# Gate/up units taken two by two in a one-core transformer block

## The chip, the cores and the metric

The kernel runs on one core of one Trainium2 chip. The metric is the device time of one execution in microseconds. Engines are called PE (TensorE; PEld is its weight load), DVE (VectorE), ACT (ScalarE), POOL (GpSimd) and SP (the engine whose queue issues the DMAs).

## The reference

One block with modulated layer norms: linear attention, then a gated feed-forward. The change lies in the feed-forward's gate and up projections. S = 2048 tokens, D = 1024, F = 3584; all inputs are bfloat16.

```python
phi = lambda t: jnp.where(t > 0, t + 1, jnp.exp(t)) + 1e-06
# linear attention A: 32 heads, num / den of phi(q), phi(k), v, then @ wo
mod = (_silu(c) @ w_mod).reshape(c.shape[0], 6, 1, -1)
sa, ca, ga, sb, cb, gb = ...
h = _layernorm(x) * (1 + ca) + sa
x = x + ga * A(h, A_wqkv, A_wo)
h = _layernorm(x) * (1 + cb) + sb
x = x + gb * (gelu(h @ w_gate) * (h @ w_up) @ w_down)
```

## The kernel before

After attention come output chunks (`wo_chunk`, 128 rows each) and then the gate/up stage, 28 units. Unit u works on half p = u // 14 of the tokens (1024 of them) and on 256 of the 3584 columns of `w_gate` and of `w_up`. Each unit is a 2 x 2 block product with seven products instead of eight (the Strassen-Winograd scheme): products 1 and 2 take the blocks as they are, in bfloat16; products 3 to 7 take sums of blocks, held in float32r. Every product is made twice, for t = 0 (gate) and t = 1 (up), with 4 matmuls of 128x128 by 512 columns each (`prod`, L1458). So a unit has 16 bfloat16 and 40 float32r matmuls, in the order 1, 2, 6, 5, 7, 3, 4.

The names and lines that matter:

- The sums of token blocks (`SS`, `s_sum`, L1413) are made once per half. The sums of weight blocks (`TP[0]` to `TP[4]`, `t_sum`) are made in each unit: numbers 0, 1, 2, 4 on DVE (L1433), number 3 is a copy on ACT (`brcp`, L1423). Sum 0 belongs to product 5, 1 to 6, 2 to 7, 3 to 3, 4 to 4; each has one buffer, so a sum for the next unit waits for the product that reads the old one. Units 1 to 27: sums 2 and 4 of the unit itself are queued behind its first product, sums 0, 1 and 3 of the next unit behind products 5, 7 and 3.
- PSUM has eight banks; a unit uses four pairs of them (t = 0 and 1): `BA` for products 1 and 2, `BB`, `BE`, `BC`. Product 1 is copied from `BA` to `BB` by ACT (`pcp`, L1463), and product 2 then adds onto `BA`. Product 6 adds onto `BB`, and `ucp` (ACT, L1473) copies that to `BC`. Product 5 goes to `BE`, from there to SBUF (`escp`, ACT, L1466), and `pinc` (DVE, L1476) adds it to `BC`. Product 7 adds onto `BB`, and `padd` (DVE, L1469) sums `BB` and the copy into `BE`. Products 3 and 4 add onto `BC` and `BB`. All four pairs then hold gate (t = 0) and up (t = 1) of one output block.
- `gelu` (ACT, L1481) takes the gate bank into one of two buffers `ge`; `y_out` (DVE, L1488) multiplies it with the up bank into `ys`. The last `y_out` of a unit is held back until the next unit's first product has been issued. `y_store` (SP, L1494) writes `ys` out.
- `wt_dma(u + 2)` loads the next but one unit's weights into one of two buffers, gate and up 512 KB each (SP, L1371). Before, it is queued behind product 2, and waits for the sums that read the old weights.
- Work for other stages is hooked into the units. `ACTS` holds, for units 2 to 11, two groups of ACT steps: squares with a running sum (`ln2_stats`, L674), followed on POOL by `ve`, `rs` and `nm` (L676, L677, L679), normalizations (`ln2_rows`, L660, which need `rs` and `nm`, and a DMA transpose after them), modulations (`act_mod`, L753) and copies. `DVES` holds POOL means, DVE sums (`s_sum`) for the second half of the tokens, and from unit 15 on the weight sums `d_t` (L1621) of the down projection. `DMAS` holds loads and stores. Before, the DMAs, the `DVES` step and the first ACT group stand behind a unit's product 2, the second ACT group behind product 5.
- Units 0 and 27 have orders of their own; unit 27 carries the first steps of the down projection (`d_t`, `d_s`, `d_first`).

Each engine's queue is in program order; what waits for what is worked out from the bytes and banks that the steps touch. A planner (`Sched.reorder`) rearranges DVE, ACT and POOL alone, and only in the stretch from output chunk 3 to the end of unit 1.

Of the kernel before, what the change touches and what calls it, by code (L numbers as in the profile page):

```python
# [7 lines left out]
ACTF = mybir.ActivationFunctionType  # L8
ALU = mybir.AluOpType

P = 128
# [12 lines left out]
NFP = NFC // 2  # L24
# [10 lines left out]
OFF_YT = OFF_HT + NSG * 8192  # L35
# [295 lines left out]
def bass_adaLN_cond__linear_attn_block__geglu_ffn__prompt_kernel(  # L331
# [18 lines left out]
    with ExitStack() as es:  # L350
# [6 lines left out]
        def at(name, shape, dty, off):  # L357
            return nc.alloc_sbuf_tensor_at(name, shape, dty, offset=ABASE + off, align_bytes=4)
# [28 lines left out]
        YS = [at(f"ys{i}", [P, CPG, 2, 2 * P], bf16, OFF_YS[i]) for i in range(3)]  # L387
        YA = [at(f"ya{r}", [P, NDJ, 2 * P], bf16, o_) for r, o_ in enumerate(OFF_YA)]
        DE = at("de", [P, 512], f32, OFF_DE)
        PK = [at(f"pk{i}", [P, D], bf16, OFF_PK[i]) for i in range(NCH)]  # L390
        MB = [at(f"mb{i}", [P, D], bf16, OFF_MB[i]) for i in range(NG)]
        MTB = [at(f"mtb{i}", [P, NDC, P], bf16, OFF_MTB[i]) for i in range(2)]
# [141 lines left out]
        def r_2k(off, name):  # L534
            return [(off, off + 2048, name)]
# [16 lines left out]
        sch = Sched()  # L552
# [815 lines left out]
        def wt_dma(u):  # L1368
            i, f0 = u % 2, u % NFP * 256
            for t, v_ in enumerate((wg_v, wu_v)):  # L1370
                sch.dma(Q, lambda e, t=t, v_=v_: e.dma_start(WT[i][:, t, :, :], v_[:, :, f0:f0 + 256]), wr=r_wt(i, t, t + 1), note=f"wt{t} u{u}")  # L1371

        def wo_chunk(c_, b0):
            wo_mm(c_, b0, list(range(NG)))
# [58 lines left out]
            sch.op(V, lambda e: e.tensor_tensor(TP[k][:], in0, in1 if k in (0, 2) else in1[:], ALU.subtract), rd=r0 + r1, wr=r_tp(k),  # L1433
                   deps=[x1_ops[7]] if u == 0 and k == 0 else [], note=f"tsum{k} u{u}")

        BA, BE, BB, BC = 0, 2, 4, 6
        gi = [0]

        def prod(u, t, k):
            p = PS_[0] = u // NFP  # L1440
            if k in (1, 2):
                r = k - 1
                lhs = lambda dc: (WT[u % 2][:, t, r * ND2 + dc, 0:P], r_wt(u % 2, t, t + 1, r * ND2 + dc, r * ND2 + dc + 1))
                rhs = lambda dc: (H2[p][0][:, r * ND2 + dc, :], r_h2(0, r * ND2 + dc, r * ND2 + dc + 1))
            else:
                ti = {5: 0, 6: 1, 7: 2, 3: 3, 4: 4}[k]
                lhs = lambda dc: (TP[ti][:, t, dc, :], r_tp(ti, t, t + 1))
                if k == 4:
                    rhs = lambda dc: (A22R[p][:, dc, :], r_ar(dc, dc + 1))
                else:  # L1450
                    si = {5: 0, 6: 1, 7: 2, 3: 3}[k]
                    rhs = lambda dc: (SS[p][si][:, dc, :], r_ss(si, dc, dc + 1))
            b = {1: BA, 2: BA, 5: BE, 6: BB, 7: BB, 4: BB, 3: BC}[k] + t
            fresh = k in (1, 5)
            o = None
            for dc in range(ND2):
                (l_, rl), (r_, rr) = lhs(dc), rhs(dc)
                o = sch.op(T, lambda e, l_=l_, r_=r_, dc=dc: e.matmul(PS(b), l_, r_, start=fresh and dc == 0, stop=dc == ND2 - 1, skip_group_check=True),  # L1458
                           rd=rl + rr, pwr=(pr(b) if dc == 0 else ()), note=f"ffn u{u} P{k} {t} dc{dc}", overwrite_ok=True)
            pset_writer(b, o)  # L1460

        def pcp(t):
            sch.op(A, lambda e: e.activation(PS(BB + t), PS(BA + t), ACTF.Copy), prd=pr(BA + t), pwr=pr(BB + t), note="pcp")  # L1463

        def escp(t):
            sch.op(A, lambda e: e.activation(ES[t][:, :], PS(BE + t), ACTF.Copy), prd=pr(BE + t), wr=r_2k(OFF_ES[t], f"es{t}"), note="escp")  # L1466

        def padd(t, dst):
            sch.op(V, lambda e: e.tensor_tensor(PS(dst + t), PS(BB + t), ES[t][:, :], ALU.add), prd=pr(BB + t), rd=r_2k(OFF_ES[t], f"es{t}"),  # L1469
                   pwr=pr(dst + t), note="padd")  # L1470

        def ucp(t):
            sch.op(A, lambda e: e.activation(PS(BC + t), PS(BB + t), ACTF.Copy), prd=pr(BB + t), pwr=pr(BC + t), note="ucp")  # L1473

        def pinc(t):
            sch.op(V, lambda e: e.tensor_tensor(PS(BC + t), PS(BC + t), ES[t][:, :], ALU.add), prd=pr(BC + t), rd=r_2k(OFF_ES[t], f"es{t}"),  # L1476
                   pwr=pr(BC + t), note="padd")

        def gelu(b):
            i = gi[0] % 2  # L1480
            sch.op(A, lambda e: e.activation(GE[i][:, :], PS(b), ACTF.Gelu_apprx_tanh), prd=pr(b), wr=r_2k(OFF_GE[i], f"ge{i}"), note="gelu")  # L1481
            gi[0] += 1
# [14 lines left out]

        held = [None]

        def unit(u, order=(1, 2, 6, 5, 7, 3, 4)):  # L1500
            more = u + 1 < 2 * NFP
            for k in order:
                if isinstance(k, tuple):
                    wo_chunk(*k)
                    continue
                if callable(k):
                    k()
                    continue
                late = u == 0 and k == 2
                gb_, gk, yt, yh = (None, 1, 0, 0) if late else {2: (BA, 0, 0, 0), 7: (BE, 1, 1, 1), 3: (BC, 0, 1, 0), 4: (BB, 0, 0, 1)}.get(k, (None, 1, 0, 0))  # L1510
                for t in range(2):
                    prod(u, t, k)
                    if k == 1:
                        if held[0]:
                            held[0]()
                            held[0] = None
                        pcp(t)
                    elif k == 5:
                        escp(t)
                        if u:  # L1520
                            pinc(t)
                    elif k == 6:
                        if u:
                            ucp(t)
                        else:
                            padd(t, BC)
                    elif k == 7:
                        padd(t, BE)
                    if gb_ is not None and t == gk:
                        gelu(gb_)  # L1530
                        ig = (gi[0] - 1) % 2
                if k == 2 and u + 2 < 2 * NFP:
                    wt_dma(u + 2)
                if k == 4:
                    def last(ig=ig):
                        y_out(ig, BB, u, 0, 1)
                        y_store(u)
                    held[0] = last
                elif gb_ is not None:
                    y_out(ig, gb_, u, yt, yh)  # L1540
                if k == 1:
                    if u == 0:
                        ar_copy(0)
                    else:
                        if u == 1:
                            t_sum(u, 1)
                        t_sum(u, 2)
                        t_sum(u, 4)
                if more:
                    if k == (3 if u == 0 else 5):  # L1550
                        t_sum(u + 1, 0)
                    if k == 7 and u:
                        t_sum(u + 1, 1)
                    if k == 3:
                        t_sum(u + 1, 3)
# [242 lines left out]
        def lat(*f):  # L1798
            return lambda: [g() for g in f]
# [34 lines left out]
        for u in range(2 * NFP):  # L1834
            if u == 0:
                unit(u, ORD0)
            elif u == 2 * NFP - 1:
                unit(u, (1, lambda: (d_t(0, 3), d_s(0, 0, (0,)), d_s(0, 1, (0,))), 2, lambda: (wd_dma(4), wd_dma(5)), 6, 5, 7,
                         lambda: (d_t(1, 3), d_s(0, 0, (1,)), d_s(0, 1, (1,))), 3, lambda: (wd_dma(6), x_in(0, 0, 1, 2, 3)), d_first, lambda: (d_t(2, 3), d_t(3, 3)), 4))
# [3 lines left out]
            if u == 1:  # L1843
                mark.append(sch.n)
        held[0]()
        held[0] = None
        def hook0(k):
# [137 lines left out]
```

## Time and profile before

| what | value |
|---|---|
| median of 3 runs | 782.76 us (782.47 to 783.43) |
| span of the profiled execution | 780.9 us |
| PE busy / DVE busy / ACT busy | 770.2 / 645.9 / 374.6 us |
| granted PE clock | full in every slice |
| gate/up matmuls (L1458), share of the chain that ended last | 45% |
| one steady unit | 12.56 us, in it DVE 10.80 to 11.93, ACT 6.73 busy |

The span runs from the first to the last instruction of one execution; the profile page gives no other time of that execution, and the median of the runs stands 1.9 us above its span. A busy time is the union of an engine's instructions; matmuls overlap, so their spacing from start to start, and not their duration, tells what PE can do.

### The profile page before, as it was taken

How to read it: one execution, taken by the hardware profiler on the slowest of the kernel's cores; microseconds unless marked ns; L12 is line 12 of the kernel's file. 1: busy time of each engine (PE TensorE's matmuls, PEld its weight loads, DVE VectorE, ACT ScalarE, POOL GpSimd, SP SyncE). 2: the span in 40 equal slices, each digit the busy share in tenths (PEclk: the TensorE clock that was granted, in tenths of full speed). 3: DMA queues.
4: the chain of work that ended last, by engine and by line, in shares of the span. 5: the costliest groups of instructions: out<-in, count | busy, mean ns of one | idle time of the engine just before them, and what ended most of it. 6: DMA issues, size and time to landing. Idle time of an engine off the chain costs nothing.

```text
span 780.9 us, 10753 instructions
## 1 busy us (share of the span) xinstructions
PE 770.2 (99%) x3825; PEld 496.2 (64%) x3883; DVE 645.9 (83%) x964; ACT 374.6 (48%) x629; POOL 47.5 (6%) x126
## 2 busy tenths in 40 slices
PE   8999999999999999999999999999999999999998
PEld 4444445666445667667676767667676576677766
DVE  6699988897899878787989888888989888676767
ACT  2497743242466487878755555555555211111111
POOL 2031300000321011100000000000000000000000
PEclk9999999999999999999999999999999999999999
DMA  9879749939999358867353865535356334443331
GB/s 284 256 167 252 158 91 215 255 80 196 203 287 231 82 138 212 230 175 215 99 145 108 250 211 172 148 96 161 97 147 221 111 127 139 144 141 114 126 125 60
DMA packets 196940, 130.22 MB, mean 167 GB/s; under 512 B 69516, under 2 KB 182420, under 8 KB 195864
## 3 DMA queue, kind: packets, MB, share of 16 engines
q1 hardware_dynamic: 196872, 129.55, 62.4%
q8 instruction: 30, 0.49, 0.3%
q14 instruction: 22, 0.18, 0.1%
q10 hardware_dynamic: 16, 0.00, 0.0%
HBM read 92.55 MB, written 23.35 MB: 148 GB/s over the span
## 4 chain that ended last, share of the span: by engine, by line
PE 95%; SPq 2%; DMA 1%; DVE 1%; issue 1%; ACT 0%; DVEq 0%; ACTq 0%
PE ps_all L1458 45%; PE ps_all L1672 21%; PE ps_all L895 7%; PE ps_all L934 7%; PE ps_all L1283 7%; PE ps_all L880 5%; PE ps_all L1593 1%; SPq L598 1%; DMA wmq<-in_w_mod_dram 1%; SPq L603 1%; DMA h1T<-xh 0%; PE ps_all L913 0%; PE ps_all L1201 0%; PE ps_all L1240 0%; DVE h1T L724 0%
## 5 line engine op out<-in xcount | busy, mean ns | idle before, releaser
L1458 PE MATMUL ps_all<-ss,tp 128*128 128x512 f32 x896 | 214.3, 396 | 0.0
L1458 PEld LDWEIGHTS ps_all<-ss,tp 128*128 128x128 f32 x896 | 168.3, 188 | 37.8 <-DVE ss L1413 0.2
L1672 PE MATMUL ps_all<-dt,sb 128*128 128x512 f32 x424 | 102.5, 398 | 0.0
L1481 ACT ACTIVATE ge<-ps_all 128x512 f32<-128x512 f32 x112 | 64.1, 597 | 73.8 <-DVE ps_all L1469 62.1
L1458 PE MATMUL ps_all<-h2a,wt 128*128 128x512 bf16 x421 | 95.7, 379 | 1.8
L1672 PEld LDWEIGHTS ps_all<-dt,sb 128*128 128x128 f32 x424 | 79.6, 188 | 18.5 <-DVE sb L1648 0.3
L1476 DVE TENSOR_TENSOR ps_all<-ps_all,es 128x512 f32<-128x512 f32 x54 | 37.6, 699 | 49.4 <-ACT es L1466 49.0
L1488 DVE TENSOR_TENSOR ys<-ge,ps_all 128x512 bf16<-128x512 f32 x112 | 74.4, 684 | 3.8 <-PE ps_all L1672 0.5
L1458 PEld LDWEIGHTS ps_all<-h2a,wt 128*128 128x128 bf16 x448 | 38.0, 98 | 57.3 <-ACT ps_all L1463 16.9
L1433 DVE TENSOR_TENSOR tp<-wt 128x1024 fp32r<-128x1024 bf16 x56 | 68.1, 1217 | 1.8 <-DMA wt<-in_B_w_up_dram 1.8
L1433 DVE TENSOR_TENSOR tp<-wt,tp 128x1024 fp32r<-128x1024 bf16 x56 | 68.2, 1218 | 0.0
L934 PE MATMUL ps_all<-h1T,wq 128*128 128x512 bf16 x256 | 56.7, 379 | 0.0
L880 PE MATMUL ps_all<-wk,h1T 128*128 128x512 bf16 x239 | 55.3, 379 | 1.1 <-DMA wk<-in_A_wqkv_dram 0.5
L1283 PE MATMUL ps_all<-w,pq 128*128 128x512 bf16 x249 | 55.7, 379 | 0.5 <-issue 0.2
L1458 PE MATMUL ps_all<-ar,tp 128*128 128x512 f32 x224 | 55.5, 390 | 0.0
L869 ACT ACTIVATE eb<-ps_all 128x512 f32<-128x512 f32 x64 | 36.3, 594 | 37.6 <-PE ps_all L880 16.0
L1672 PE MATMUL ps_all<-wd,ya 128*128 128x512 bf16 x199 | 47.5, 380 | 0.7
L1458 PEld LDWEIGHTS ps_all<-ar,tp 128*128 128x128 f32 x224 | 42.1, 188 | 8.9
L1463 ACT ACTIVATE ps_all<-ps_all 128x512 f32<-128x512 f32 x56 | 32.6, 582 | 26.8 <-PE ps_all L1458 26.5
L934 PEld LDWEIGHTS ps_all<-h1T,wq 128*128 128x128 bf16 x256 | 25.0, 98 | 30.0
L1283 PEld LDWEIGHTS ps_all<-w,pq 128*128 128x128 bf16 x256 | 24.6, 98 | 30.3 <-issue 1.1
L1643 ACT ACTIVATE sb<-ya 128x896 fp32r<-128x896 bf16 (+1 forms) x16 | 14.5, 913 | 58.8 <-PE ps_all L1672 58.8
(141 smaller groups left out, 976.3 us busy)
## 6 DMA issues: line engine op xcount, KB each, us to landing
wt<-in_B_w_gate_dram SPq DMA_DIRECT2D x28, 512.0 KB, 4.0
wt<-in_B_w_up_dram SPq DMA_DIRECT2D x28, 512.0 KB, 5.2
scr_y<-ys SPq DMA_DIRECT2D x28, 512.0 KB, 3.2
ya<-scr_y SPq DMA_DIRECT2D x14, 896.0 KB, 4.9
rb<-scr_rd SPq DMA_DIRECT2D x32, 256.0 KB, 6.0
wd<-in_B_w_down_dram SPq DMA_DIRECT2D x7, 1024.0 KB, 7.6
wmst<-in_w_mod_dram SPq DMA_DIRECT2D x6, 1024.0 KB, 6.2
wmq<-in_w_mod_dram SPq DMA_DIRECT2D x8, 512.0 KB, 7.5
```

The source lines that it names most:

```text
L869: sch.op(A, lambda e: e.activation(EB[i][:, :], PS(bank), ACTF.Exp), prd=pr(bank), wr=rng, note=f"{note}.exp")
L880: o = sch.op(T, lambda e, dc=dc: e.matmul(PS(bank), H1[sg][:, ci, dc, :], W_[:, dc, jg * 512:(jg + 1) * 512], start=(dc == 0), stop=(dc == ...
L895: o = sch.op(T, lambda e, c_=c_: e.matmul(PS(bank, 0, n), PK[c_][:, g * P:(g + 1) * P], xrow(c_, o_, o_ + n), start=(c_ == 0), stop=(c_ == ...
L934: o = sch.op(T, lambda e, dc=dc: e.matmul(PS(b), WQ[:, dc, qc * P:(qc + 1) * P], H1[sg][:, :, dc, :], start=(dc == 0), stop=(dc == NDC - 1 ...
L1283: last[half] = sch.op(T, lambda e, g=g, half=half: e.matmul(PS(b0 + half), PQ[sg][:, g, ci * P:(ci + 1) * P], W2[:, g, half * 512:(half + ...
L1433: sch.op(V, lambda e: e.tensor_tensor(TP[k][:], in0, in1 if k in (0, 2) else in1[:], ALU.subtract), rd=r0 + r1, wr=r_tp(k), deps=[x1_ops[7 ...
L1458: o = sch.op(T, lambda e, l_=l_, r_=r_, dc=dc: e.matmul(PS(b), l_, r_, start=fresh and dc == 0, stop=dc == ND2 - 1, skip_group_check=True) ...
L1463: sch.op(A, lambda e: e.activation(PS(BB + t), PS(BA + t), ACTF.Copy), prd=pr(BA + t), pwr=pr(BB + t), note="pcp")
L1476: sch.op(V, lambda e: e.tensor_tensor(PS(BC + t), PS(BC + t), ES[t][:, :], ALU.add), prd=pr(BC + t), rd=r_2k(OFF_ES[t], f"es{t}"), pwr=pr( ...
L1481: sch.op(A, lambda e: e.activation(GE[i][:, :], PS(b), ACTF.Gelu_apprx_tanh), prd=pr(b), wr=r_2k(OFF_GE[i], f"ge{i}"), note="gelu")
L1488: sch.op(V, lambda e: e.tensor_tensor(YS[s_][:, 2 * h:2 * h + 2, t, :], q(GE[i][:, :]), q(PS(b + 1)), ALU.mult), rd=r_2k(OFF_GE[i], f"ge{i ...
L1672: o = sch.op(T, lambda e, l_=l_, r_=r_, j=j, dst=dst: e.matmul(dst, l_[:, 0, :], r_, start=(k in (1, 5) or own is not None) and j == js[0] ...
```

## The change

Units 1 to 26 are taken as pairs (1, 2), (3, 4) up to (25, 26); a is the first unit of a pair and b the second. The order of products is a1, a2, b1, b2 (bfloat16), then a6, a5, a7, a3, a4, b6, b5, b7, b3, b4 (float32r). Units 0 and 27 stay alone.

- Banks: each pair has its own assignment, handed on from pair to pair; a's `C` shares the pair of banks of its `A`, b's `A` and `B` are the same pair, `E` is shared. b's first product is parked in SBUF (`ppark`, to `pb`) and copied back to PSUM (`pback`) behind a's third product. Unit 0 and the output chunks 6 to 8 get other banks.
- Weight sums for b: 0 behind a's product 5; 1 behind the two additions of a's product 7 and ahead of that product's `y_out` (`mid`); 2 behind that `y_out`; 3 (ACT) behind the copies back; 4 behind b's product 6.
- `wt_dma` for b + 2 moves behind b's product 6 and its sum 4.
- Hooks of a: the DMAs behind its product 2, the `DVES` step and the first ACT group behind b's product 1, the second ACT group behind a's product 5. Hooks of b: the DMAs behind its product 6; the `DVES` step behind b's product 5 for b < 9, else behind b's product 7 and the next unit's sum 1; both ACT groups behind b's product 5.
- The `s_sum` steps of the second half move into units 11, 12 and 13 (before: 11 to 14).

```diff
+OFF_PB = [OFF_YT + 53248, OFF_YT + 55296]
...
-        BA, BE, BB, BC = 0, 2, 4, 6
+        BA, BE, BB, BC = 6, 0, 2, 4
+        MAIN = dict(A=BA, B=BB, E=BE, C=BC)
...
+        def ppark(t, m):
+            sch.op(A, lambda e: e.activation(PB[t][:, :], PS(m["A"] + t), ACTF.Copy), prd=pr(m["A"] + t), wr=r_pb(t), note="pcp")
+
+        def pback(t, m):
+            sch.op(A, lambda e: e.activation(PS(m["B"] + t), PB[t][:, :], ACTF.Copy), rd=r_pb(t), pwr=pr(m["B"] + t), note="pcp")
...
+        def step(u, k, m, park=False, mid=None):
...
+            for t in range(2):
+                prod(u, t, k, m)
+                if held[0]:
+                    held[0]()
+                    held[0] = None
+                if k == 1:
+                    (ppark if park else pcp)(t, m)
+                elif k == 5:
+                    escp(t, m)
+                    if u:
+                        pinc(t, m)
...
+                elif k == 7:
+                    padd(t, m, m["E"])
+                if gb_ is not None and t == gk:
+                    gelu(gb_)
+                    ig = (gi[0] - 1) % 2
...
+            if mid:
+                mid()
+            if gb_ is not None and k != 4:
+                y_out(ig, gb_, u, yt, yh)
...
+        def pair(a, w, hook):
+            b = a + 1
+            ma = dict(A=w[0], B=w[2], E=w[1], C=w[0])
+            mb = dict(A=w[3], B=w[3], E=w[1], C=w[0])
+            step(a, 1, ma)
+            if a == 1:
+                t_sum(a, 1)
+            t_sum(a, 2)
+            t_sum(a, 4)
+            step(a, 2, ma)
+            wt_next(a)
+            hook(a, 0)
+            step(b, 1, mb, True)
+            hook(a, 1)
+            hook(a, 2)
+            step(b, 2, mb)
+            for k in (6, 5, 7, 3, 4):
+                step(a, k, ma, mid=(lambda: t_sum(b, 1)) if k == 7 else None)
+                if k == 5:
+                    t_sum(b, 0)
+                    hook(a, 3)
+                elif k == 7:
+                    t_sum(b, 2)
+                elif k == 3:
+                    for t in range(2):
+                        pback(t, mb)
+                    t_sum(b, 3)
+            if a == 1:
+                mark.append(sch.n)
+            for k in (6, 5, 7, 3, 4):
+                step(b, k, mb)
+                if k == 6:
+                    t_sum(b, 4)
+                    wt_next(b)
+                    hook(b, 0)
+                elif k == 5:
+                    t_sum(b + 1, 0)
+                    if b < 9:
+                        hook(b, 1)
+                    hook(b, 2)
+                    hook(b, 3)
+                elif k == 7:
+                    t_sum(b + 1, 1)
+                    if b > 8:
+                        hook(b, 1)
+                elif k == 3:
+                    t_sum(b + 1, 3)
+            return w[2], w[3], w[1], w[0]
...
-                wo_chunk(c_, 2 * (c_ % 4))
+                wo_chunk(c_, (0, 0, 4, 6, 0, 2, 6, 4, 6, 0, 2, 4, 6, 0)[c_])
...
-        DVES[11] = ss(1, 0)
-        DVES[12] = lat(ss(1, 1), ss(2, 0))
-        DVES[13] = ss(2, 1)
-        DVES[14] = lat(ss(3, 0), ss(3, 1))
+        DVES[11] = lat(ss(1, 0), ss(1, 1))
+        DVES[12] = lat(ss(2, 0), ss(2, 1))
+        DVES[13] = lat(ss(3, 0), ss(3, 1))
...
+        def hook(u, n):
+            if n == 0:
+                DMAS.get(u, nop)()
+            elif n == 1:
+                DVES.get(u, nop)()
             else:
-                a = ACTS.get(u, ((), ()))
-                unit(u, (1, 2, lat(DMAS.get(u, nop), DVES.get(u, nop), *a[0]), 6, 5, lat(*a[1]), 7, 3, 4))
...
+                lat(*ACTS.get(u, ((), ()))[n - 2])()
+
+        unit(0, ORD0)
+        w_ = (BA, BB, BE, BC)
+        for u in range(1, 2 * NFP - 1, 2):
+            w_ = pair(u, w_, hook)
+        MAIN = dict(zip("ABEC", w_))
+        assert w_ == (0, 4, 2, 6)
...
```

The ACT groups of the units, unchanged, as far as they are used below:

```python
ACTS[2] = (sq(12), sq(13)), (xh(12),)
ACTS[4] = (xh(14), xh(15)), (sq(8),)
ACTS[6] = (sq(10), sq(11)), (xh(10),)
ACTS[8] = (mo(1, 3, 4, 5),), (mo(1, 6, 7),)
ACTS[10] = (mo(0, 4, 5, 6),), (mo(0, 7),)
```

Here `sq` is a square, `xh` a normalization and `mo` one modulation for each number behind the first.

More of the change, by code (lines that the diff above doesn't have):

```diff
@@ L389, in bass_adaLN_cond__linear_attn_block__geglu_ffn__prompt_kernel @@
         DE = at("de", [P, 512], f32, OFF_DE)
+        PB = [at(f"pb{i}", [P, 512], f32, OFF_PB[i]) for i in range(2)]
         PK = [at(f"pk{i}", [P, D], bf16, OFF_PK[i]) for i in range(NCH)]
@@ L1452, in prod @@
                     rhs = lambda dc: (SS[p][si][:, dc, :], r_ss(si, dc, dc + 1))
-            b = {1: BA, 2: BA, 5: BE, 6: BB, 7: BB, 4: BB, 3: BC}[k] + t
+            b = m[{1: "A", 2: "A", 5: "E", 6: "B", 7: "B", 4: "B", 3: "C"}[k]] + t
             fresh = k in (1, 5)
@@ L1460, in prod, with r_pb, pcp, escp @@
             pset_writer(b, o)
[L1462 to L1469, printed above, removed]
-                   pwr=pr(dst + t), note="padd")
[L1472 to L1477, printed above, removed]
+        def r_pb(t):
+            return r_2k(OFF_PB[t], f"pb{t}")
+        def pcp(t, m):
+            sch.op(A, lambda e: e.activation(PS(m["B"] + t), PS(m["A"] + t), ACTF.Copy), prd=pr(m["A"] + t), pwr=pr(m["B"] + t), note="pcp")
+        def ppark(t, m):
+            sch.op(A, lambda e: e.activation(PB[t][:, :], PS(m["A"] + t), ACTF.Copy), prd=pr(m["A"] + t), wr=r_pb(t), note="pcp")
+        def pback(t, m):
+            sch.op(A, lambda e: e.activation(PS(m["B"] + t), PB[t][:, :], ACTF.Copy), rd=r_pb(t), pwr=pr(m["B"] + t), note="pcp")
+        def escp(t, m):
+            sch.op(A, lambda e: e.activation(ES[t][:, :], PS(m["E"] + t), ACTF.Copy), prd=pr(m["E"] + t), wr=r_2k(OFF_ES[t], f"es{t}"), note="escp")
+        def padd(t, m, dst):
+            sch.op(V, lambda e: e.tensor_tensor(PS(dst + t), PS(m["B"] + t), ES[t][:, :], ALU.add), prd=pr(m["B"] + t), rd=r_2k(OFF_ES[t], f"es{t}"),
+                   pwr=pr(dst + t), note="padd")
+        def ucp(t, m):
+            sch.op(A, lambda e: e.activation(PS(m["C"] + t), PS(m["B"] + t), ACTF.Copy), prd=pr(m["B"] + t), pwr=pr(m["C"] + t), note="ucp")
+        def pinc(t, m):
+            sch.op(V, lambda e: e.tensor_tensor(PS(m["C"] + t), PS(m["C"] + t), ES[t][:, :], ALU.add), prd=pr(m["C"] + t), rd=r_2k(OFF_ES[t], f"es{t}"),
+                   pwr=pr(m["C"] + t), note="padd")
         def gelu(b):
@@ L1498, in bass_adaLN_cond__linear_attn_block__geglu_ffn__prompt_kernel, with last, wt_next, unit @@
         held = [None]
-        def unit(u, order=(1, 2, 6, 5, 7, 3, 4)):
+        def step(u, k, m, park=False, mid=None):
+            late = u == 0 and k == 2
+            gb_, gk, yt, yh = (None, 1, 0, 0) if late else {2: (m["A"], 0, 0, 0), 7: (m["E"], 1, 1, 1), 3: (m["C"], 0, 1, 0), 4: (m["B"], 0, 0, 1)}.get(k, (None, 1, 0, 0))
+            for t in range(2):
[9 more added lines that the diff above has]
+                        pinc(t, m)
+                elif k == 6:
+                    if u:
+                        ucp(t, m)
+                    else:
+                        padd(t, m, m["C"])
+                elif k == 7:
[3 more added lines that the diff above has]
+                    ig = (gi[0] - 1) % 2
+            if k == 4:
+                def last(ig=ig):
+                    y_out(ig, m["B"], u, 0, 1)
+                    y_store(u)
+                held[0] = last
+            if mid:
+                mid()
+            if gb_ is not None and k != 4:
+                y_out(ig, gb_, u, yt, yh)
+        def wt_next(u):
+            if u + 2 < 2 * NFP:
+                wt_dma(u + 2)
+        def unit(u, order):
             more = u + 1 < 2 * NFP
@@ L1508, in unit @@
                     continue
[L1509 to L1540, printed above, removed]
+                step(u, k, MAIN)
+                if k == 2:
+                    wt_next(u)
                 if k == 1:
@@ L1544, in unit @@
                     else:
-                        if u == 1:
-                            t_sum(u, 1)
                         t_sum(u, 2)
                         t_sum(u, 4)
[L1549 to L1555, printed above, removed]
+                if more and k == 3:
+                    t_sum(u + 1, 0)
+                    t_sum(u + 1, 3)
+        def pair(a, w, hook):
[46 more added lines that the diff above has]
+            return w[2], w[3], w[1], w[0]
         def x_out(i):
```

12 lines of the change are left out of this document (3 added, 9 removed).

## The prediction

> **What bounds the kernel now.** I read the page first: busy shares, granted clock, chain.
>
> ```profile
> PE 770.2 (99%) x3825; PEld 496.2 (64%) x3883; DVE 645.9 (83%) x964; ACT 374.6 (48%) x629; POOL 47.5 (6%) x126
> PEclk9999999999999999999999999999999999999999
> PE 95%; SPq 2%; DMA 1%; DVE 1%; issue 1%; ACT 0%; DVEq 0%; ACTq 0%
> ```
>
> TensorE (PE) is nearly never idle, at full clock, and is 95% of the chain. So nothing off PE can gain; the change gains only by making PE's own stream denser, and loses wherever PE must wait. Next, PE's timeline over a unit:
>
> ```profile
> 412.13 3.40 PE L1458 MATMUL ps_all<-h2a,wt 128*128 128x512 bf16 x15
> 415.18 7.63 PE L1458 MATMUL ps_all<-ss,tp 128*128 128x512 f32 x32
> 422.65 1.98 PE L1458 MATMUL ps_all<-ar,tp 128*128 128x512 f32 x8
> 424.69 3.40 PE L1458 MATMUL ps_all<-h2a,wt 128*128 128x512 bf16 x15
> ```
>
> A unit takes 424.69 - 412.13 = 12.56 us, the same in all steady units: there are no stalls to remove. (One of 16 bf16 records is missing in each unit, always the first; it starts 0.216 before the second, at 424.48, so the float32r half begins 16 x 0.2158 later, at 427.93.) Then the waits around the first product's copy `pcp` (L1463), and the weight load behind it:
>
> ```profile
> L1463 ACT ACTIVATE ps_all<-ps_all x56: 582/582/582, 242.5 to 589.8; 128x512 f32<-128x512 f32 x56
> ...
>   PEld ps_all L1458: 16.9, 56
> ```
> ```profile
> 426.17 0.35 PEld L1458 LDWEIGHTS ps_all<-h2a,wt 128*128 128x128 bf16 x3 [0.30 <-ACT ps_all L1463]
> ```
>
> This is the row that matters. The second product accumulates onto the bank that the copy reads, so it waits for the copy. All 56 copies hold the weight load (0.30 us each), and the load goes at 426.17 for a matmul due at 426.20. The copy is hidden with 0.02 to 0.03 us to spare: an ACT that comes later to it stops PE by nearly the whole delay. So I read ACT's queue around it:
>
> ```profile
> 431.78 0.60 ACT L1466 ACTIVATE es<-ps_all 128x512 f32<-128x512 f32 x1 [0.31 <-PE ps_all L1458]
> 434.88 1.09 ACT L1481 ACTIVATE ge<-ps_all 128x512 f32<-128x512 f32 x2 [2.50 <-DVE ps_all L1469]
> 435.85 1.15 ACT L1423 ACTIVATE tp<-wt 128x512 fp32r<-128x512 bf16 x2
> 436.89 0.60 ACT L1481 ACTIVATE ge<-ps_all 128x512 f32<-128x512 f32 x1
> ...
> 438.10 0.58 ACT L1463 ACTIVATE ps_all<-ps_all 128x512 f32<-128x512 f32 x1 [0.61 <-PE ps_all L1458]
> ```
>
> From the second `escp` (431.78) to the next unit's first copy (438.10) are 6.32 us. ACT needs 0.49 for the `escp`, then, from the first gelu on, 2.01 to the last gelu (436.89 - 434.88) and 0.50 for it. Room for anything else: 6.32 - 0.49 - 2.51 = 3.32 us.
>
> **The change, part by part.** Times are worked on the unit above; a is a pair's first unit, b its second.
>
> *Fewer switches.* Matmuls start 0.2158 apart in bf16 and 0.2267 in float32r: 16 and 40 of them are 3.45 + 9.07 = 12.52, so switching there and back costs 0.04 a unit. Thirteen pairs save one each: -0.52 us.
>
> *b's float32r half.* It follows a's directly (9.07 us). Its pincs, padds and escps stand in the old order. In a's half: the padds start at 434.15 and 434.75, so the sum moved behind them runs 435.36 to 436.58, and b's sixth product begins at 427.93 + 9.07 = 437.0: hidden, 0.4 spare. The copies back (`pback`) go behind the two gelus, 435.85 and 436.36, ended by 436.94 at most; they are needed at 437.0 and 437.9 (the first one is done at 436.43): hidden. brcps and last gelu slip by 1.0, with nobody waiting. Vector engine (DVE) from 435.36, by its spacings (1.135 a sum, 0.60 an addition or output): sum, output, sum, two outputs, sum, ending its issue at 440.57; b's first `pinc` is due at 431.51 + 9.07 = 440.58. So the queue just closes up, and b's padds keep the old 0.34 us ahead of the fourth product. Cost 0, price if not: third rival.
>
> *DMA.* b's next weights are requested after its fourth sum, about 440.7 (gate) and 441.2 (up), and land 4.0 and 5.2 later, at 446.4 the latest; needed by the next b's first product at 446.1 + 3.45 = 449.55. a's keep their place. SP issues in the same order as before; outputs, transposes and the wd loads move with their step. Hidden by some 3 us; if a load came 4 us late, PE would stand by 1 in that pair.
>
> *Banks.* Output chunk 8 now reuses chunk 6's bank; that was read out at 217.65 + 1.22 = 218.87, chunk 8 begins at about 220.7. No cost. b's copies to `pb` write SBUF as `escp` does, 0.598 against 0.582: 0.016 longer, inside the 0.02 to 0.03. I take 0; the upper bound is 26 x 0.016 = 0.42. The Trainium skill (ScalarE: Activation LUTs, Step-by-step) says writing PSUM is the faster way out of ScalarE, which speaks against parking in SBUF; the rows agree in sign. With the skill's fixed costs (Perfetto Trace Analysis, Optimizing Scalar/DVE Operations: some 93 ns SBUF, 51 PSUM) the copy would be 0.042 longer, and the sum 26 x (0.042 - 0.02) = 0.6 us higher, at 785.4, an estimate.
>
> *ACT hooks of b.* Formerly b's normalization steps were split: one group behind the second product, one behind the fifth. Now, for b, both groups stand behind the fifth product's sums, that is inside the 3.32 us of room:
> - Unit 4: two normalizations and a square, 1.133 us each (302.13 x2 to 304.39; 294.08 with its accumulator read): 3.40, over by 0.08; minus the spare 0.02, a stall of 0.06.
> - Unit 8: five modulations at 0.705 (352.40 x3 to 354.52): 3.53, over by 0.21, stall 0.19. Unit 10: four, 2.82, fits.
> - Units 2 and 6: two squares, then a normalization that needs GpSimd's (POOL's) result for the first. This distance can be read from a square that stood behind the fifth product:
>
> ```profile
> 294.08 1.14 ACT L674 ACTIVATE xl<-xall,mv 128x1024 bf16<-128x1024 bf16 x1
> ```
> ```profile
> 295.47 0.62 POOL L676 TENSOR_SCALAR ve<-st 128x1 f32<-128x1 f32 x1 [2.28 <-ACT xl L674]
> 296.18 0.56 POOL L677 TENSOR_TENSOR rs<-ve,neghalf 128x1 f32<-128x1 f32 x1
> 296.81 0.20 POOL L679 TENSOR_TENSOR nm<-mv,rs 128x1 f32<-128x1 f32 x1
> ```
>
> 297.01 - 294.08 = 2.93, plus 0.05 to hand over, plus 1.13 for the normalization: 4.11, over by 0.79, stall 0.77 each, 1.54 for both. The 0.62 of `ve` is 0.19 elsewhere (278.39); here it ends with a DVE weight sum (294.83 + 1.22 = 296.05), and after the change the same sum stands at the same place. With 0.19 the stall would be 0.34 each. The Trainium skill (SBUF — State Buffer, Who interferes with whom) has DVE and GpSimd share a port pair under an exclusive lock; by that rule, the trace agrees, the long form is the one to expect.
>
> Each stall is at the next pair's second product; behind it ACT catches up. a's hooks run beside bf16 matmuls and delay only a gelu and the `ucp`s, by up to 0.9 of 1.9 spare (429.05 + 0.58 against the seventh product at 431.56).
>
> *The seam to unit 27.* In b, the DVE hook (one sum of `wd`) is queued ahead of the unit's last two outputs:
>
> ```profile
> 586.94 1.22 DVE L1433 TENSOR_TENSOR tp<-wt,tp 128x1024 fp32r<-128x1024 bf16 x1
> 588.07 1.28 DVE L1488 TENSOR_TENSOR ys<-ge,ps_all 128x512 bf16<-128x512 f32 x2
> ```
> ```profile
> 589.75 0.58 ACT L1463 ACTIVATE ps_all<-ps_all 128x512 f32<-128x512 f32 x1 [0.28 <-PE ps_all L1458]
> ```
>
> The second output starts at 588.67 and lasts 0.68. Shifted by 1.14 it ends at 590.49. In other pairs nothing near waits for it, but unit 27 copies its first product into that very bank: its second copy goes at 590.52 instead of 589.75, stall 0.77 - 0.02 = 0.75. (Without it, the same shift would bring the first `pinc` 0.5 late.)
>
> Sum: -0.52 + 0.06 + 0.19 + 1.54 + 0.75 = +2.0. The profiled execution spans 780.9 (so 782.9 after); the median of the runs, 782.76, is 1.9 above it, and I add the change to the median: 784.8. What a measurement here can tell from no change is about 0.2%, 1.57 us.
>
> **The rivals.**
> 1. *The switch saving alone* (not slower): ACT and DVE absorb every seam, since their queues have idle time in sum (48% and 83% busy). It gives 782.76 - 0.52 = 782.2. Against it: the 56 held weight loads. It decides if the copies have more slack than 0.03 us.
> 2. *POOL quick*: as mine, with 0.19 for `ve`: 784.8 - 2 x 0.43 = 783.9.
> 3. *DVE too tight in every pair*: the chain that closes up at 440.57 has no slack but the 0.35 ahead of the padds. If waits between engines break its overlap, so that four sums and three outputs take their durations (1.22, 0.68) and not their spacings, it is 7 x 0.085 = 0.6 later, and PE stalls 0.25 in 13 pairs: 784.8 + 3.2 = 788.0. For it: the order is new; against it: the spacings held back to back in every unit before.
> 4. *Faster*: the 0.45 between the last float32r (422.65 + 1.98 - 0.39 = 424.24) and the first recorded bf16 matmul (424.69) holds a true gap of 0.23, and 13 go: 782.76 - 3.0 = 779.8 before any stall. Against it: one of 16 records is missing just there.
>
> **How the numbers follow.** My forecast 0.52, its own range 784.0 to 785.6 (modulations cheaper, `pb` copies up to 0.42); rival 1 0.17, rival 2 0.15, rival 3 0.13, rival 4 0.03. Slower by over 0.2% is above 784.33: nearly all of mine (0.48) and rival 3, 0.61. Within: 0.04 + 0.17 + 0.15 = 0.36. Faster (below 781.19): 0.03. The range 782.1 to 786.4 takes in rivals 1 and 2 and the mild part of rival 3.
>
> **What would show it.** After: pairs of 25.08 us on PE; `pcp` as releaser of PE matmuls, with idle time, at four seams (units 3, 5, 7, 9) and in unit 27; the first copy of units 3 and 7 some 0.8 late. I am wrong if the stage is gapless there, if gaps of one size recur in all pairs, or if PE waits for `wt`.

## The result, and the profile after

The changed kernel takes 784.70 us (median of 9 runs, 784.43 to 785.57). The kernel before took 782.76 in the 9 runs beside it; the ratio is 1.0027, 95% interval 1.0017 to 1.0036. The profiled execution spans 782.8 against 780.9. So the change is slower by 1.9 us, as forecast, and by the forecast's size; of the forecast's terms one, the saving by fewer switches, was twice too large.

The page of the changed kernel, first the lines that answer to those of before, then the row of PE's bfloat16 products (busy time, mean ns, idle time ahead and its releaser):

```profile
PE 774.1 (99%) x3883; PEld 496.8 (63%) x3883; DVE 643.9 (82%) x964; ACT 386.9 (49%) x655; POOL 48.6 (6%) x126
...
PEclk9999999999999999999999999999999999999999
...
L1461 PE MATMUL ps_all<-h2a,wt 128*128 128x512 bf16 x448 | 100.0, 380 | 1.8 <-ACT ps_all L1469 1.8
```

The clock is full as before. PE's busy sum is higher by 3.9 us only because the record of before lacks some matmuls (3825 of them against 3883). What is new is the last row: PE itself now stands idle for 1.8 us by this view, released by the first product's copy `pcp` (now L1469). Before, the copies held only weight loads.

PE's timeline over one steady pair (start, duration, matmuls in a row):

```profile
413.18 7.08 PE L1461 MATMUL ps_all<-h2a,wt 128*128 128x512 bf16 x32
419.91 7.65 PE L1461 MATMUL ps_all<-ss,tp 128*128 128x512 f32 x32
427.40 1.98 PE L1461 MATMUL ps_all<-ar,tp 128*128 128x512 f32 x8
429.21 7.42 PE L1461 MATMUL ps_all<-ss,tp 128*128 128x512 f32 x32
436.47 1.98 PE L1461 MATMUL ps_all<-ar,tp 128*128 128x512 f32 x8
438.28 1.90 PE L1461 MATMUL ps_all<-h2a,wt 128*128 128x512 bf16 x8
```

Both units' bfloat16 products stand in one run of 32, then 80 in float32r: 438.28 - 413.18 = 25.10 us a pair, where two units took 2 x 12.56 = 25.12. The saving is 0.02 a pair, not the 0.04 of the forecast.

Now the copies, in the view of one line's instructions and who waited for them:

```profile
L1469 ACT ACTIVATE ps_all<-ps_all x30: 567/582/604, 242.3 to 591.7; 128x512 f32<-128x512 f32 x30
...
who waited for it (us, times):
  PEld ps_all L1461: 10.7, 27
  PE ps_all L1461: 1.8, 3
```

Three of the waits are now PE's own, and these are the large ones. Call extra spacing the distance from one matmul's start to the next above its usual 0.216 (bfloat16) or 0.227 (float32r). In the bfloat16 runs it is 0.749 us in unit 3, 0.041 in unit 5, 0.731 in unit 7, 0.160 in unit 9 and 0.806 in unit 27, always at the second product, 2.49 in sum. The stage's other waits are three in units 0 and 27, and the kernel before has them too (3.37, 3.39 and 1.55 us in both). The seam from unit 2 to unit 3, in the timeline of all engines:

```profile
281.28 1.14 ACT L676 ACTIVATE xl<-xall,mv 128x1024 bf16<-128x1024 bf16 x1
...
282.02 1.22 DVE L1435 TENSOR_TENSOR tp<-wt 128x1024 fp32r<-128x1024 bf16 x1
...
282.66 0.62 POOL L678 TENSOR_SCALAR ve<-st 128x1 f32<-128x1 f32 x1 [22.94 <-ACT xl L676]
...
284.02 0.19 POOL L681 TENSOR_TENSOR nm<-mv,rs 128x1 f32<-128x1 f32 x1
...
284.24 1.24 ACT L662 ACTIVATE xl<-xall,nm,rs 128x1024 bf16<-128x1024 bf16 x1 [0.59 <-POOL nm L681]
...
286.03 1.90 PE L1461 MATMUL ps_all<-h2a,wt 128*128 128x512 bf16 x8
...
287.86 1.08 ACT L1469 ACTIVATE ps_all<-ps_all 128x512 f32<-128x512 f32 x2
...
288.52 2.33 PE L1461 MATMUL ps_all<-h2a,wt 128*128 128x512 bf16 x10 [0.58 <-ACT ps_all L1469]
```

Here is the chain of the forecast, step by step: first square, the slow `ve` beside the weight sum, `nm`, a normalization that waits 0.59 for it, the gelus, and a `pcp` that starts 1.83 after the pair's first matmul where 1.08 is its place when nothing holds it (589.96 against 588.88 at unit 27's first copy). PE starts its second product 0.75 late. And unit 27:

```profile
589.14 1.22 DVE L1685 TENSOR_TENSOR dh<-wd,dt 128x1024 fp32r<-128x1024 bf16 x1
...
590.28 1.28 DVE L1500 TENSOR_TENSOR ys<-ge,ps_all 128x512 bf16<-128x512 f32 x2
...
591.65 0.58 ACT L1469 ACTIVATE ps_all<-ps_all 128x512 f32<-128x512 f32 x1 [1.11 <-PE ps_all L1461]
...
592.29 1.04 PE L1461 MATMUL ps_all<-h2a,wt 128*128 128x512 bf16 x4 [0.64 <-ACT ps_all L1469]
```

The `wd` sum pushes the last two outputs, the second ends at 590.28 + 1.28 = 591.56, and 0.09 later the second copy starts. The timeline names PE as the copy's releaser, but PE's matmul for it had ended by 590.8. The real releaser is the output, which reads the bank that the copy overwrites.

The difference of the two profiled spans, 1.90, adds up within 0.01 as: stalls +2.49; the switch saving 13 x 0.02 = -0.26; three gaps of 0.034, 0.048 and 0.019 that the execution of before had in this stage, -0.10; and -0.22 ahead of unit 1 (its first matmul at 260.93 against 261.15). That last term isn't the change's: in the runs below the same matmul starts anywhere from 260.4 to 262.3. So the text reads distances inside the stage, and medians for times.

### The profile page after: what moved, and what is told of

The parts are those of the page before. It is cut to its first block, busy times and chain, and to the rows that moved or that the text cites. A ratio compares the mean times of both kernels' runs of the same rounds, so it can differ in the third digit from the quotient of the medians.

```text
span 782.8 us, 10890 instructions
## 1 busy us (share of the span) xinstructions
PE 774.1 (99%) x3883; PEld 496.8 (63%) x3883; DVE 643.9 (82%) x964; ACT 386.9 (49%) x655; POOL 48.6 (6%) x126
## 4 chain that ended last, share of the span: by engine, by line
PE 56%; ACT 0%; DVE 0%; DVEq 0%; issue 0%
PE ps_all L1461 34%; PE ps_all L1736 21%; PE ps_all L1657 1%; ACT ps_all L1469 0%; ACT tp L1425 0%; ACT ge L1493 0%; DVE ps_all L1640 0%; DVE xq L1641 0%; DVEq L351 0%; DVEq L2008 0%
## 5 line engine op out<-in xcount | busy, mean ns | idle before, releaser
L1461 PE MATMUL ps_all<-ss,tp 128*128 128x512 f32 x896 | 211.7, 393 | 0.0
L1461 PE MATMUL ps_all<-h2a,wt 128*128 128x512 bf16 x448 | 100.0, 380 | 1.8 <-ACT ps_all L1469 1.8
L1478 ACT ACTIVATE es<-ps_all 128x512 f32<-128x512 f32 x56 | 33.5, 598 | 17.1 <-PE ps_all L1461 16.8
```

The lines of the kernel that those rows point to most:

```text
L1478: sch.op(A, lambda e: e.activation(ES[t][:, :], PS(m["E"] + t), ACTF.Copy), prd=pr(m["E"] + t), wr=r_2k(OFF_ES[t], f"es{t}"), note="escp")
```

## The experiments

Each is an edit of the changed kernel, and the ratio after each time is to the kernel before. Beside the runs of the first four, the kernel before took 783.01 us, beside the next four 782.83 and beside the last two 782.94, against 782.76 beside the changed kernel. So what an edit changes is told below by the distances to the kernel before, which is 1.94 for the changed kernel.

**Unit 27's seam alone** (e1_unit27): the hook of unit 26 with the `wd` sum moves to the bfloat16 part of the pair.

```diff
             step(b, 2, mb)
+            if b == 26:
+                hook(b, 1)
...
-                    if b > 8:
+                    if 8 < b < 26:
                         hook(b, 1)
```

> Edit: the changed kernel, with the DVE weight sum hooked into unit 26 moved from ahead of that unit's last outputs to the end of its pair's bfloat16 half. Theory (unit 27's second copy waits for an output that this sum delayed): the 1.02 us gap in unit 27's bfloat16 run goes, the four other gaps (0.75, 0.04, 0.73 and 0.16 beyond the usual spacing) stay, span 782.8 - 0.8 = 782.0, time 783.9. Rival (unit 27 is late for another reason, such as its new banks or the copies themselves): the gap stays, 784.7.

Measured: 784.44 us, ratio 1.0016 (1.0007 to 1.0025). Its timeline at unit 27:

```profile
589.45 1.28 DVE L1500 TENSOR_TENSOR ys<-ge,ps_all 128x512 bf16<-128x512 f32 x2
...
591.12 0.58 ACT L1469 ACTIVATE ps_all<-ps_all 128x512 f32<-128x512 f32 x1 [0.28 <-PE ps_all L1461]
```

The outputs end at 590.72, the copy starts on time (0.86 behind the first, as PE delivers the banks), and unit 27's gap is gone; the four others are there (0.755, 0.043, 0.741, 0.162). The place and mechanism are shown. The distance to the kernel before is 1.43, so the time fell by 0.5 where 0.8 was expected; the interval of the ratio is 0.7 us to either side and can't tell these apart. In the profiled executions the way from unit 1's first matmul to the end is shorter by 0.97 (520.95 against 521.92).

**ScalarE's groups alone** (e2_groups): the same squares, normalizations and modulations, regrouped so that the second unit of each pair carries no more than fits, and none waits for POOL there.

```diff
-        ACTS[2] = (sq(12), sq(13)), (xh(12),)
-        ACTS[3] = (xh(13), sq(14)), (sq(15),)
-        ACTS[4] = (xh(14), xh(15)), (sq(8),)
-        ACTS[5] = (sq(9), xh(8)), (xh(9),)
-        ACTS[6] = (sq(10), sq(11)), (xh(10),)
-        ACTS[7] = (xh(11), mo(1, 0, 1)), (mo(1, 2),)
-        ACTS[8] = (mo(1, 3, 4, 5),), (mo(1, 6, 7),)
+        ACTS[2] = (sq(12), sq(13)), ()
+        ACTS[3] = (xh(12), xh(13)), (sq(14), sq(15))
+        ACTS[4] = (xh(14), xh(15)), ()
+        ACTS[5] = (sq(8), sq(9)), (xh(8), xh(9))
+        ACTS[6] = (sq(10), sq(11)), ()
+        ACTS[7] = (xh(10), xh(11)), (mo(1, 0, 1, 2, 3),)
+        ACTS[8] = (mo(1, 4, 5),), (mo(1, 6, 7),)
```

> Edit: the changed kernel, with the ACT groups spread anew over units 2 to 8: no second unit of a pair has more than two squares or normalizations or four modulations behind its fifth product, no step is left out. Theory (ACT has 3.32 us of room there, and what goes beyond it delays the next pair's first copy): the gaps of units 3, 5, 7 and 9 go, unit 27's 0.8 stays, span 782.8 - 1.7 = 781.1, time 783.0. Rival (the pairs' seams are late in themselves while the stage's early transfers run): gaps stay where they are, 784.7.

Measured: 783.31 us, ratio 1.0004 (0.9995 to 1.0013). The copies' line:

```profile
who waited for it (us, times):
  PEld ps_all L1461: 9.9, 30
  PE ps_all L1461: 0.6, 1
```

One wait of PE is left, that of unit 27 (extra spacing 0.805); the four seams are clean. The distance to the kernel before is 0.30, so the time fell by 1.64 where 1.7 was expected. So what ScalarE carried in those four places made them.

**Both** (e3_both), the two edits together.

> Edit: both edits, the moved DVE sum and the spread ACT groups. Theory: no gap is left in the gate/up stage, pairs of 25.10 us throughout, span 780.3 to 780.5, time 782.2 to 782.4: 0.3 to 0.5 below the kernel before, which is what fewer switches are worth (13 times 0.02 to 0.04). Rival (fewer switches are worth nothing, the longer bfloat16 runs cost it elsewhere): 782.8 or more.

Measured: 782.52 us, ratio 0.9995 (0.9986 to 1.0004); none of the five extra spacings is left, and a pair takes 25.10 throughout. By the distances to the kernel before it is 2.43 us faster than the changed kernel, which is the 2.49 of stalls within the spread. From the kernel before it can't be told apart: without its stalls the change is worth 13 x 0.02 = 0.3 us by PE's spacings and 0.5 by the medians, less than a measurement here can tell.

**POOL's share** (e4_pool): for units 3 and 7 the weight sum beside which `ve` ran moves behind the seventh product's outputs.

```diff
                 elif k == 5:
-                    t_sum(b + 1, 0)
+                    if b not in (2, 6):
+                        t_sum(b + 1, 0)
...
                 elif k == 7:
+                    if b in (2, 6):
+                        t_sum(b + 1, 0)
                     t_sum(b + 1, 1)
```

> Edit: the changed kernel, with the DVE sum 0 for units 3 and 7 moved from ahead of the additions of product 7 to behind that product's output, so that no DVE weight sum runs while POOL works on the first square's result. Theory (POOL's first step is held to the end of the DVE sum, 0.62 instead of 0.19, and the normalization waits for it): ve 0.19 in units 2 and 6, the gaps of units 3 and 7 shrink by 0.43 each to about 0.3, time 784.7 - 0.86 = 783.8. Rival (the hold does not come from DVE's sum, or ACT is not waiting for POOL): gaps unchanged, 784.7.

Measured: 784.14 us, ratio 1.0014 (1.0005 to 1.0023). The seam from unit 2 to unit 3:

```profile
284.02 0.19 POOL L678 TENSOR_SCALAR ve<-st 128x1 f32<-128x1 f32 x1 [23.03 <-ACT xl L676]
...
285.17 1.24 ACT L662 ACTIVATE xl<-xall,nm,rs 128x1024 bf16<-128x1024 bf16 x1 [0.16 <-POOL nm L681]
...
289.44 1.25 PE L1461 MATMUL ps_all<-h2a,wt 128*128 128x512 bf16 x5 [0.15 <-ACT ps_all L1469]
```

`ve` takes 0.19 without the sum beside it, the normalization waits 0.16 instead of 0.59, and the extra spacing falls from 0.749 to 0.314 in unit 3 and from 0.731 to 0.301 in unit 7: 0.43 each, the difference of the two forms of `ve`. The distance to the kernel before is 1.13, so the time fell by 0.81 where 0.86 was expected. Here `ve` runs beside an addition of `padd` (283.98 to 284.67), which reads PSUM and SBUF, and isn't held by it; the weight sum has both its inputs in SBUF. The Trainium skill (SBUF — State Buffer, Who interferes with whom) has VectorE and GpSimd lock their shared port against each other; by that rule, the trace agrees, a one-column POOL operation sits out the rest of the sum.

**The room on ScalarE, by dose** (e5_dose5, e6_dose8): extra copies in pairs that have no hooks on ScalarE there, 5 in one kernel and 8 in the other.

```diff
                     hook(b, 3)
+                    if 13 < b < 26:
+                        for _ in range(8):
+                            sch.op(A, lambda e: e.activation(PB[1][:, :], PB[0][:, :], ACTF.Copy), rd=r_pb(0), wr=r_pb(1), note="pcp")
```

> In six pairs without any normalization or modulation (second units 14, 16, 18, 20, 22 and 24), five extra ScalarE copies of 512 columns (SBUF to SBUF, some 0.5 us each by the spacing of like copies, 2.5 us in all) stand behind the fifth product's hooks of the pair's second unit, where the normalization steps of units 2, 4, 6, 8 and 10 stood. They are pure load: no other engine is asked for anything. Theory (room of 3.32 us between the second escp and the next pair's first copy): 2.5 us fit, no gap at the seams of units 15 to 25, time that of the changed kernel, 784.7 us, with the five gaps known from it. Rival (the room is smaller than the rows gave, or any ScalarE work there delays the copy): a gap at each of the six seams, up to 0.5 us each, 785 to 787.7.

> As the run with five extra copies, but with eight (some 4.0 us). Theory: they overrun the room of 3.32 us by some 0.7, less 0.02 of spare: a gap of 0.6 to 0.9 us at the second bf16 product of each of units 15, 17, 19, 21, 23 and 25, equal to eight times the copies' measured spacing minus 3.34; sum 4 to 5.5 us, time 788.5 to 790.2. Rival (ScalarE catches up elsewhere, the room is larger than 4 us): no gap there, 784.7. Second rival (the queue also holds back an earlier reader, such as the copy of the fourth product's bank): gaps in the float32r run as well, and more than 5.5 us.

Measured: 784.79 us with five, no extra spacing at any of the six seams; 795.88 us with eight. The timeline with eight, at the seam to unit 15:

```profile
434.45 5.27 ACT L1615 ACTIVATE pb<-pb 128x512 f32<-128x512 f32 x8
...
439.63 1.06 ACT L1493 ACTIVATE ge<-ps_all 128x512 f32<-128x512 f32 x2
...
442.10 1.09 ACT L1469 ACTIVATE ps_all<-ps_all 128x512 f32<-128x512 f32 x2
...
442.76 1.04 PE L1461 MATMUL ps_all<-h2a,wt 128*128 128x512 bf16 x4 [1.66 <-ACT ps_all L1469]
```

A copy cost 0.664, not 0.5: it takes 0.632 here, and each starts 0.03 after the end of the one before, whose tile it writes again. Up to the start of the gelu behind them, eight take 439.63 - 434.45 = 5.18, and PE's second product has 1.822 of extra spacing at all six seams (10.9 us; the median is 11.1 above that with five). So the room is 5.18 - 1.82 = 3.36 us, where the forecast's rows gave 3.32 and 0.02 of spare. Five take 3.19 and fit. The expected 788.5 to 790.2 was missed by the copies' price. Its formula (eight spacings minus 3.34) would give 1.97 with the spacing of 0.664; with the 5.18 that the eight really hold the queue it gives 1.84, the gap within 0.02.

**The moved weight sum** (e7_nomid): it goes back behind the seventh product's first output.

```diff
-                step(a, k, ma, mid=(lambda: t_sum(b, 1)) if k == 7 else None)
+                step(a, k, ma)
...
                 elif k == 7:
+                    t_sum(b, 1)
                     t_sum(b, 2)
```

> Undoes one part of the change alone: the second unit's weight sum number 1 goes back from behind the first unit's seventh-product additions to where the old order had it, behind the seventh-product step with its first output. It then starts after that output on VectorE, some 0.6 to 0.8 us later, and ends at about 437.3 on the steady pair's clock where it is due at 437.0 (the second unit's sixth product). Theory: PE waits 0.3 to 0.5 us at the start of the second unit's float32r half in each of the 13 pairs, as it reads that sum: +4 to +6.5 us, time 788.7 to 791.2; what follows on VectorE is late by nothing more, since the queue holds the same work. Rival: the sum has more room than the rows say, no wait, 784.7.

Measured: 792.02 us, ratio 1.0118 (1.0102 to 1.0133). The timeline at the start of a second unit's float32r half:

```profile
430.82 0.69 DVE L1500 TENSOR_TENSOR ys<-ge,ps_all 128x512 bf16<-128x512 f32 x1
...
431.42 1.22 DVE L1435 TENSOR_TENSOR tp<-wt,tp 128x1024 fp32r<-128x1024 bf16 x1
...
432.69 2.14 PE L1461 MATMUL ps_all<-ss,tp 128*128 128x512 f32 x8 [0.24 <-DVE tp L1435]
```

The sum ends at 432.64; PE was due at 432.29 and starts at 432.69, 0.40 late, as expected. But a pair takes 25.63 to 25.68, that is 0.53 to 0.58 more: the second matmul follows 0.341 behind the first (0.114 more than usual), and the next few 0.01 each. A wait in a float32r run costs 0.13 to 0.18 on top of itself. That is why 792.0 lies above the range.

**The copies' slack** (e8_small): a copy of 8 columns ahead of each parking copy, from the same bank.

```diff
         def ppark(t, m):
+            sch.op(A, lambda e: e.activation(PB[t][:, 0:8], PS(m["A"] + t, 0, 8), ACTF.Copy), prd=pr(m["A"] + t), wr=r_pb(t), note="pcp")
```

> A small ScalarE copy (8 columns, PSUM to SBUF; one column took 0.17 us and eight 0.21 elsewhere in this trace) stands ahead of each of the 26 parking copies of the pairs' second units and reads the same bank. It makes each of those copies later by its own spacing, some 0.1 to 0.2 us, and changes nothing else. Theory (the copy of a first product ends only 0.02 to 0.03 us before PE needs the bank): PE stands by the spacing less 0.02 to 0.03 at the second product, 26 times 0.08 to 0.18, +2 to +4.7 us, time 786.8 to 789.4. Rival (the wait of the weight load is cheap and the copies have slack of 0.1 us or more): no gap in PE's stream, 784.7.

Measured: 787.76 us, ratio 1.0061 (1.0046 to 1.0076). The timeline at one second unit:

```profile
444.37 0.18 ACT L1472 ACTIVATE pb<-ps_all 128x8 f32<-128x8 f32 x1 [1.05 <-PE ps_all L1461]
444.58 0.60 ACT L1473 ACTIVATE pb<-ps_all 128x512 f32<-128x512 f32 x1
445.23 0.54 PEld L1461 LDWEIGHTS ps_all<-h2a,wt 128*128 128x128 bf16 x4 [0.53 <-ACT pb L1473]
445.24 0.18 ACT L1472 ACTIVATE pb<-ps_all 128x8 f32<-128x8 f32 x1
...
446.09 0.33 PEld L1461 LDWEIGHTS ps_all<-h2a,wt 128*128 128x128 bf16 x3 [0.32 <-ACT pb L1473]
```

The parking copy is late by 0.209 and PE's second product by 0.197 (0.198 in some pairs): the slack is 0.012 us. That is the 0.02 to 0.03 read before less the 0.015 by which a parking copy is longer (0.597 for 0.582), so those copies cost nothing, but barely. But PE stands once a pair, 13 times, not 26: its stop at the first bank also moves the time at which it needs the second, whose copy was not moved by that stop. Thirteen times 0.21 (pairs of 25.31) is 2.7; by the distances to the kernel before the time rose by 3.0. That it lies in the expected range is in part luck: there were half as many stops as expected, each a little larger than the largest expected.

**VectorE's queue, by dose** (e9_v1, e10_v2): extra additions of 512 columns in six pairs, behind the second unit's sum 3 (which is ScalarE's). On VectorE they run ahead of that unit's last weight sum, number 4, which is queued behind its product 6, and so ahead of its first pinc, where the forecast had the queue just close up.

```diff
...
                     t_sum(b, 3)
+                    if 13 < b < 26:
+                        for _ in range(2):
+                            sch.op(V, lambda e: e.tensor_tensor(PB[1][:, :], PB[0][:, :], PB[0][:, :], ALU.add), rd=r_pb(0), wr=r_pb(1), note="padd")
```

> In six pairs (second units 14 to 24, even), one extra VectorE addition of 512 float32 columns in SBUF (some 0.6 us by the spacing of like additions) stands behind the last weight sum for the second unit, ahead of its first pinc, where the forecast had the queue just close up (440.57 against 440.58). Theory: the first pinc is late by the full 0.6, but the second one waits for its escp 0.2 longer anyway, so it and the padds are late by some 0.3 to 0.4; they stand 0.34 ahead of the fourth product, so PE waits 0 to 0.05 in each of the six, time within 0.3 of the changed kernel's 784.7. Rival (the third of the forecast: the queue is too tight in every pair): PE already depends on the pinc or the padds without spare, and each of the six pairs is 0.4 to 0.6 longer, 787 to 788.5.

> As the run with one extra VectorE addition, but with two (some 1.2 us). Theory: the padds are late by 0.9 to 1.0, less 0.34 of spare: PE waits 0.5 to 0.7 ahead of the second unit's fourth product (or at the third, if that reads them sooner) in each of six pairs, and loses some 0.1 to 0.2 more as it takes up a float32r run after a wait (0.16 in the run with the late weight sum): +3.6 to +5.4, time 788.3 to 790.1. Rival (the sums behind the pincs have slack too, and the queue recovers before anyone waits): no gap, 784.7.

Measured: 784.99 us with one (1.0026, 1.0016 to 1.0036), 789.60 with two (1.0089, 1.0072 to 1.0106). With two, in the timeline:

```profile
433.50 1.29 DVE L1488 TENSOR_TENSOR ps_all<-ps_all,es 128x512 f32<-128x512 f32 x2
434.24 1.69 PEld L1461 LDWEIGHTS ps_all<-ss,tp 128*128 128x128 f32 x8 [0.42 <-DVE ps_all L1488]
...
435.83 1.29 DVE L1481 TENSOR_TENSOR ps_all<-ps_all,es 128x512 f32<-128x512 f32 x2
...
436.57 1.21 PE L1461 MATMUL ps_all<-ar,tp 128*128 128x512 f32 x4 [0.22 <-DVE ps_all L1481]
```

PE stops twice, at the third product for the first pinc (extra spacing 0.156, then 0.112) and at the fourth for the padds (0.378, then 0.114); the six pairs are longer by 0.8 each. With one addition the padds are 0.26 late and a pair is 0.05 to 0.10 longer, with some 0.06 of it at the second matmul of the fourth product. So the chain has room for not quite one more addition, and rival 3 begins there.

## Why the prediction was right, point by point

- *What bounds the kernel*: held. Every microsecond lost is one in which PE stood, and each was at the bank of a first product's copy. The slack of the parking copies is 0.012 by the e8 run.
- *Fewer switches, -0.52*: right in kind, mis-sized. A pair takes 25.10, not 25.08, so it was -0.26. Worked from the same spacings, a pair's matmuls need 32 x 0.2158 + 80 x 0.2267 = 25.04; switching there and back costs 0.06 in the changed kernel where a unit of before paid 0.04. It isn't a fixed price, though: in the runs with unit 27's edit alone and with the groups alone nearly all undisturbed pairs took 25.08, the forecast's value, with two additions 25.08 to 25.11, in the others 25.10, with the same order on PE; this stays open (last section).
- *b's float32r half and the moved sum, 0*: right. In the changed kernel the sum ends at 427.54 + 1.22 = 428.76 for a matmul at 429.21, 0.45 ahead (0.4 forecast); e7 shows what it costs without that.
- *The queue that closes up*: right. The last sum starts at 431.60 in the steady pair and the first pinc follows it without a gap; the first padd ends 0.36 ahead of the fourth product.
- *DMA, 0*: right; between 240 and 600 us nothing on any engine is seen to wait for a load of the gate or up weights.
- *Parked copies, 0 with 0.42 as the upper bound*: right at 0; the copies took 0.597 as forecast, and the matmuls behind them keep 0.216 to 0.217. The bound was too high: by e8 only one of a pair's two can cost, 13 x 0.016 = 0.2. The 0.6 worked from the Trainium skill (Perfetto Trace Analysis, Optimizing Scalar/DVE Operations) isn't seen: 0.597 against 0.582 is 0.015 longer, not 0.042.
- *The copies back*: hidden, though they take 0.608 each where the forecast's times supposed 0.58. The first ends at 428.65 for a matmul at 429.21.
- *ScalarE's hooks*: unit 2, 0.749 for 0.77; unit 6, 0.731 for 0.77; unit 4, 0.041 for 0.06; unit 8, 0.160 for 0.19; unit 10 fits. All are 0.02 to 0.04 below, 0.02 of it because the room is 3.36 and not 3.34.
- *Unit 27*: 0.806 for 0.75, by the output that the forecast named.
- *The sum*: +2.0 forecast, 1.9 measured. The switch term was 0.26 too favourable, and the 0.22 ahead of unit 1 and the 0.10 of small gaps go the other way: neither is in the forecast's sum, which took a unit of before as 12.56 throughout, where three were 0.02 to 0.05 longer; so the signs, places and mechanism were foreseen, while the agreement within 0.1 is in part luck. Rival 1 fell with the copies' slack, rival 2 with `ve` at 0.62, rival 3 with e9, rival 4 with the pairs of 25.10.

## What to carry to other kernels

In this kernel, whose PE has no idle time, joining runs of one type bought 0.02 to 0.04 us a pair, while moving other engines' work cost up to 0.8 where a copy or an output on a bank that PE needs next was held up; so count the slack of that one reader, and then, for the queue ahead of it, room minus load at every place where the load differs. Small extra operations put there in two doses, one that should fit and one that shouldn't, measured the room here within hundredths. And an idea and its damage can be taken apart: here the version with both edits gives the 2.4 us back and leaves a gain too small to tell.

## What the runs showed of the hardware that was not expected

- PE pays for a wait in a float32r run a second time: after the stop the second matmul follows 0.335 to 0.341 behind the first, against 0.227, and the next ones about 0.01 late each (e7, e10). After a stop in a bfloat16 run it is 0.010 once (0.226 against 0.216). The reading that a float32r weight load (0.188 against 0.098) is laid bare fits, but no run tested it.
- A float32r product whose first matmul started on time, 0.10 behind the end of the addition that it needed (e9: 436.31 behind 436.20), still lost 0.062 at its second matmul; its first weight load had been held to 436.26. A bfloat16 product lost nothing with a copy that ended 0.066 ahead (changed kernel: 443.408 for 443.474).
- The first eight or so matmuls of a float32r run are some 0.005 slow each, in sum between 0.014 and 0.051 in different places and executions with the same order of matmuls. This is what halves the switch saving; what sets it is open.
- ScalarE's copy from SBUF to PSUM takes 0.608, longer than PSUM to SBUF (0.597) or PSUM to PSUM (0.582); these are the medians of 26, 26 and 30 copies of 512 columns in the changed kernel.
